# Weight loads of the last two chunks' second layer issued by SyncE instead of ScalarE

## The chip, the cores and the metric

The kernel runs on one core of a Trainium2 chip. The metric is the time of one execution on the device in microseconds. TensorE (PE) multiplies matrices; VectorE (DVE), ScalarE (ACT) and GpSimd (POOL) work element by element; ScalarE and SyncE (SP) also issue the transfers between the chip's main memory and its on-chip memory, each in its own order of instructions.

## The reference

The kernel computes a memory attention and, on its output, a token and channel mixer, all in 32-bit floating point. Cut to what matters:

```python
k_m = einsum("bhsm,bhsd->bhmd", softmax(phi, axis=2), k)      # likewise v_m from v
attn_out = softmax(q @ k_m.T / sqrt(64)) @ v_m                # 8 batches, 8 heads, 576 rows of 64
x = attn_out as (8, 576, 512)
h = relu(x.T @ w_tok1) @ w_tok2                               # over the 576 rows, 256 wide
u = x + h.T
out = u + relu(u @ w_ch1) @ w_ch2                             # over the 512 channels, 1536 wide
```

The change touches the last line, `relu(u @ w_ch1) @ w_ch2`, for the last two ninths of the rows.

## The kernel before

The 8 x 576 = 4608 rows are cut into nine chunks of 512, numbered 0 to 8. For each chunk the channel mixer has a first layer (512 channels to 1536 hidden values) and a second layer (back to 512). To keep 32-bit accuracy each operand is split into a high and a low part, and each product is three matmuls: high by high, high by low, low by high. The attention of later batches is computed between the channel mixer's matmuls of earlier chunks; nearly all of it is written out in the program's own order, so that every engine's instructions stand in the order in which the Python code emits them.

Chunks 0 to 2 are computed plainly. Chunks 3 to 6 take their first layer in quarters by a scheme with seven products instead of eight. The last two chunks, 7 and 8, are taken together, as a "double chunk", with both layers in that scheme. The seven products have the names "11", "21", "T2", "T1", "T3", "22", "T4", in this order.

The weights for these products are read from main memory, where an earlier part of the kernel has put them as sums of quarters. One transfer of 128 x 1024 values (512 KB), a "unit", holds the weights of two of the twelve hidden pieces of one product. The second layer of the double chunk takes 7 x 3 = 21 units, here numbered 0 to 20 (in the built program, unit_7313 is unit 0, unit_7689 is 18, unit_7711 is 19 and unit_7725 is 20). `load_unit(n)` makes a unit's tile and issues its load. The tile comes from a ring with the tag "c1", which units share with some of the hidden pieces: a load waits for the last reader of what its slot held.

The loop over `i` and `p` (L2267 to L2285) emits this second layer: for each product `name` and each hidden piece `p`,

- `double.piece` makes the split of a later hidden piece (`y` or `yT`), by a cast on ScalarE (L449, or a ReLU at L140) and a subtraction on VectorE (L450 or L143), and for T3 and T4 first a subtraction on VectorE (L439, L441);
- `load_unit(m0 + i * G + p // 2 + AHEAD)`, for every second `p`, issues the load of the unit three ahead;
- `double.second` emits the six matmuls (L456) of this piece into two of the four PSUM accumulators `e`;
- at `p == 1`, `gather` adds the accumulators that an earlier product has finished to the output tile on VectorE (L2260) and, where a half of a chunk's output is complete, stores it from SyncE (L219).

The calls of this loop load units 3 to 20. Units 0 to 2 are loaded from the first layer's loop (L2213). Product T4 comes after the loop (L2291 to L2302): it runs in three parts into the banks `end0` (512 rows of chunk 7), `end1` and `end2` (256 each), with units 18, 19 and 20 in each, and each part is added to the output (L2301) and stored (L2302).

The pieces of T4, the gathers of products T3 and T1 and the store of half of chunk 8 all come at the end of the loop. On VectorE the six T4 pieces stand ahead of these gathers, since `made` runs up to ten pieces ahead.

Of the kernel before, what the change touches and what calls it, by code (L numbers as in the profile page):

```python
# [28 lines left out]
def kernel(  # L29
# [25 lines left out]
    nc = tc.nc  # L55
# [10 lines left out]
    NF = 2 * w_ch2.shape[0]  # L66
# [9 lines left out]
    WIN, AHEAD = 3, 3  # L76
# [52 lines left out]
    def f32(t):  # L129
        return t.bitcast(F32)  # L130
# [435 lines left out]

    units = {}

    def load_unit(n):
        m = n - 2 * NF * (DOUBLE - WIN + 1)  # L570
        if m >= 7 * NF // 4:
            return
        p, j = n // 4 % (NF // 2), n % 4
        t = sb.tile([P, 1024], F32R, tag="c1", name=f"unit{n}", bufs=NF)
        if m >= 0:
            units[n] = t.rearrange("p (o x m) -> p o x m", o=2, x=2)
            nc.scalar.dma_start(out=f32(t), in_=Sums2.to[:, m // (NF // 4), m % (NF // 4)])
            return
        units[n] = t.rearrange("p (o x a n) -> p o x a n", o=2, x=2, a=2)
        m = 512 if j == 3 else 1024  # L580
        nc.scalar.dma_start(out=f32(t)[:, :m], in_=sums[p].to[:, j, :m])
# [1391 lines left out]
    while starts[-1][:2] != (B - 1, 1):  # L1973
        b, Q, m, r = starts[-1]
# [89 lines left out]
    for n in range(AHEAD):  # L2064
        at(2 * NF * WIN - 4 + n, load_unit, n, k=1)
# [50 lines left out]
    def quarters(c, p):  # L2116
# [22 lines left out]
        def product(ps, k, name, first):  # L2139
            if not k % 2:  # L2140
                load_unit(n + k // 2 + AHEAD)
            ch.product(ps, units[n + k // 2][:, k % 2], name, first, name in ("21", "22", "T4"))
# [59 lines left out]
    for p in range(NF // 2):  # L2202
        h, n = 2 * NF * DOUBLE + 4 * p, n0 + 4 * p
# [7 lines left out]
        def product(ps, k, name, first):  # L2211
            if not k % 2:
                load_unit(n + k // 2 + AHEAD)  # L2213
            double.product(ps, units[n + k // 2][:, k % 2], name, first, name in ("21", "22", "T4"))
# [34 lines left out]
    G = NF // 4  # L2249
# [4 lines left out]
    m0 = n0 + 2 * NF  # L2254
    after = []

    def gather(t, m, ps, store):
        for a in range(2):
            o = oc[t].o[:, 2 * m + a]
            nc.vector.tensor_tensor(out=o, in0=ps[a], in1=o, op=ALU.add)  # L2260
        if store:
            oc[t].store(channels=slice(2 * m, 2 * m + 2))
# [4 lines left out]
    for i, name in enumerate(double.order[:-1]):  # L2267
        y = name in ("21", "T1", "22")
        for p in range(NF // 2):
            k = i * (NF // 2) + p  # L2270
            while made[0] <= min(k + (6 if k < NF // 2 else 10), len(pieces) - 1):
                double.piece(*pieces[made[0]])
                made[0] += 1
            if not p % 2:
                load_unit(m0 + i * G + p // 2 + AHEAD)
            for a in range(2):
                double.second(
                    chain[y][a], a, name, p, units[m0 + i * G + p // 2][:, p % 2],
                    p == 0 and name in ("11", "21", "T1"), p == NF // 2 - 1,
                )  # L2280
            if p == 1:
                for x in after:
                    gather(*x)
                after.clear()
        after += [(t, m, chain[y], z) for t, m, z in ends[i]]  # L2285
# [100 lines left out]
```

## Time and profile before

| What | Value |
|---|---|
| median of 3 runs | 750.62 us (749.58 to 751.95) |
| profiled execution, whole | 751.26 us |
| its span in the profile | 749.5 us |
| ScalarE busy | 343.5 us (46%) |
| loads at L577 (second layer's units), issued by ScalarE | 21 of 512 KB |

The span is what the profile shows of the execution. Names such as `unit<-sums` are the program's tiles without their numbers: the target, an arrow, the source. `sums` is the store of weight sums in main memory, `u` the output tiles of chunks 7 and 8. PEld is TensorE's weight load, which runs beside the matmuls; ACTq and SPq are the instruction queues of ScalarE and SyncE, where transfers are issued. A row of the timeline gives start and duration in microseconds, then engine, line, operation, target and source, sizes, how many were merged into the row, and in brackets the idle time before it and what ended it. Merged rows overlap.

### The profile page before, as it was taken

To read this page: it belongs to the slowest core of one execution; us is meant where nothing else is said; L and a number is where in the kernel's file an instruction comes from. 1 tells how busy PE (TensorE), PEld (TensorE's weight loads), DVE (VectorE), ACT (ScalarE), POOL (GpSimd) and SP (SyncE) were. 2 spreads that over 40 slices of the span, in tenths; PEclk is the share of its full clock that TensorE was granted. 3 is DMA by queue.
4 is the path that set the end of the run, shared out by engine and by line. 5 is a ranking of instruction groups with operands and counts; after the bars stand their busy time and mean duration, and the time that the engine had idled before them with its cause. 6 is when DMAs were issued, how large, how long until landed. Compare 5 with 4: busy or idle time off the path is not lost.

```text
span 749.5 us, 12863 instructions
## 1 busy us (share of the span) xinstructions
PE 738.3 (99%) x4883; PEld 631.4 (84%) x4883; DVE 514.5 (69%) x920; ACT 343.5 (46%) x740; POOL 104.7 (14%) x90
## 2 busy tenths in 40 slices
PE   9999999999999999999999999999999999999997
PEld 8677788787878888898898889889898998888886
DVE  4989884787657768875577748675766555655874
ACT  5897554242314243545354536354444452444430
POOL 2134443012032021120010102010101000000000
PEclk9999999999999999999999999999999999999999
DMA  8945630584824554879596968878577555776654
GB/s 346 414 183 199 224 120 1 133 259 145 276 67 115 211 140 140 284 223 321 170 293 215 285 229 233 288 225 309 158 235 213 198 151 174 254 251 211 223 170 169
DMA packets 98462, 158.34 MB, mean 211 GB/s; under 512 B 42208, under 2 KB 65632, under 8 KB 94304
## 3 DMA queue, kind: packets, MB, share of 16 engines
q1 hardware_dynamic: 77808, 91.05, 36.8%
q10 hardware_dynamic: 20592, 66.46, 27.7%
q8 instruction: 39, 0.64, 0.3%
q14 instruction: 23, 0.19, 0.1%
HBM read 121.57 MB, written 35.91 MB: 210 GB/s over the span
## 4 chain that ended last, share of the span: by engine, by line
PE 57%; DVE 8%; DMA 5%; ACT 2%; SPq 1%; issue 1%; POOL 0%; ACTq 0%; DVEq 0%; POOLq 0%
PE acc L198 18%; PE qa L336 7%; PE qb L336 5%; PE u L937 5%; PE e L456 4%; PE da L401 4%; PE db L401 3%; PE cp L175 3%; PE Ap L897 2%; DMA rows<-S 1%; DMA raw<-rows 1%; PE sp L755 1%; PE sp L656 1%; PE end L456 1%; DMA sums<-c1h 1%; DMA sums<-sums 1%
## 5 line engine op out<-in xcount | busy, mean ns | idle before, releaser
L198 PE MATMUL acc<-qhh,c 128*128 128x512 f32 x256 | 99.8, 395 | 0.0
L198 PE MATMUL acc<-hh,c 128*128 128x512 f32 x288 | 96.5, 394 | 0.0
L336 PEld LDWEIGHTS qa<-xT,unit 128*128 128x128 f32 x432 | 60.7, 188 | 8.6 <-ACT whole L2134 2.9
L336 PEld LDWEIGHTS qb<-x,unit 128*128 128x128 f32 x432 | 60.9, 188 | 8.2 <-ACT whole L2134 2.2
L198 PEld LDWEIGHTS acc<-hh,c 128*128 128x128 f32 x288 | 54.1, 188 | 14.1 <-issue 2.7
L336 PE MATMUL qa<-xT,unit 128*128 128x256 f32 x432 | 63.5, 282 | 0.8 <-ACT whole L2134 0.7
L336 PE MATMUL qb<-x,unit 128*128 128x256 f32 x432 | 63.2, 282 | 0.9 <-ACT whole L2134 0.9
L2137 DVE TENSOR_TENSOR whole<-whole 128x256 f32<-128x256 f32 x48 | 26.1, 543 | 52.4 <-ACT whole L2134 52.1
L828 POOL TENSOR_TENSOR a<-aT,a 64x576 fp32r<-64x576 f32 x22 | 33.5, 1523 | 175.0 <-ACT a L827 152.3
L198 PE MATMUL acc<-hl,c 128*128 128x512 f32 x144 | 56.2, 390 | 0.0
L198 PEld LDWEIGHTS acc<-qhh,c 128*128 128x128 f32 x256 | 48.2, 188 | 9.2 <-issue 3.3
L198 PE MATMUL acc<-qal,c 128*128 128x512 f32 x192 | 54.7, 394 | 0.0
L2134 ACT COPY whole<-qa 128x256 f32<-128x256 f32 x72 | 26.9, 374 | 53.4 <-PE qa L336 44.9
L175 PE MATMUL cp<-uh,c1h 128*128 128x512 f32 x144 | 51.3, 397 | 0.0
L198 PE MATMUL acc<-qhl,c 128*128 128x512 f32 x128 | 50.8, 396 | 0.0
L175 PE MATMUL cp<-ul,c1h 128*128 128x512 f32 x144 | 50.3, 390 | 0.0
L175 PE MATMUL cp<-uh,c1l 128*128 128x512 f32 x144 | 50.2, 389 | 0.0
L143 DVE SCALAR_TENSOR_TENSOR hl<-cp,hh 128x512 fp32r<-128x512 f32 x36 | 24.7, 687 | 36.5 <-ACT hh L140 36.4
L198 PEld LDWEIGHTS acc<-qal,c 128*128 128x128 f32 x192 | 32.3, 189 | 3.0
L140 ACT ACTIVATE hh<-cp 128x512 fp32r<-128x512 f32 x36 | 21.5, 597 | 26.1 <-PE cp L175 26.0
L937 PE MATMUL u<-w2h,Rl 128*128 128x288 f32 x112 | 33.0, 295 | 0.3 <-DVE Rl L143 0.3
L2134 ACT COPY whole<-qb 128x256 f32<-128x256 f32 x48 | 17.8, 370 | 33.9 <-PE qb L336 33.7
(284 smaller groups left out, 1713.3 us busy)
## 6 DMA issues: line engine op xcount, KB each, us to landing
unit<-sums ACTq DMA_DIRECT2D x111, 512.0 KB, 4.2
kv<-in_kv_dram SPq DMA_DIRECT2D x12, 1280.0 KB, 8.0
rawc<-in_w_ch_dram SPq DMA_DIRECT2D x12, 1024.0 KB, 10.1
q<-in_q_dram SPq DMA_DIRECT2D x16, 576.0 KB, 7.3
unit<-sums ACTq DMA_DIRECT2D x30, 256.0 KB, 3.7
sums<-sums SPq DMA_DIRECT2D x12, 512.0 KB, 6.1
sums<-v SPq DMA_DIRECT2D x12, 512.0 KB, 5.5
phi<-in_phi_dram SPq DMA_DIRECT2D x16, 320.0 KB, 3.9
```

The lines of the kernel that those rows point to most:

```text
L140: nc.scalar.activation(out=h, in_=ps, func=AF.Relu)
L143: nc.vector.scalar_tensor_tensor(out=l, in0=ps, scalar=0.0, in1=f32(h), op0=ALU.max, op1=ALU.subtract)
L175: nc.tensor.matmul(ps, l[:, a, w], r[:, a], start=n == 0, stop=n == len(mm) - 1)
L198: nc.tensor.matmul(ps, l_[f // 2][:, f % 2, a * P : (a + 1) * P], r[:, w], start=f == start and x == 0, stop=f == end - 1 and x == 2,)
L336: nc.tensor.matmul(ps[:, :HW], l, r, start=first and n == 0, stop=n == len(mm) - 1, skip_group_check=not first,)
L401: nc.tensor.matmul(ps, l, r, start=first and n == 0, stop=n == len(mm) - 1, skip_group_check=not first,)
L456: nc.tensor.matmul(ps, weights[:, x, m], r[:, w], start=first and n == 0, stop=last and n == 2, skip_group_check=name in ("T2", "T3", "22"),)
L828: s.low_eng.tensor_tensor(out=l, in0=s.aT[own], in1=f32(h), op=ALU.subtract)
L897: nc.tensor.matmul(ps[:, :TT], a, w, start=x == 0, stop=x == len(mm) - 1)
L937: nc.tensor.matmul(ps[:, :HALF], a, r, start=x == 0, stop=x == len(mm) - 1)
L2134: nc.scalar.copy(out=to, in_=ps[:, :HW])
L2137: nc.vector.tensor_tensor(out=to, in0=x, in1=y, op=ALU.add)
```

## The change

`load_unit` gets a second argument, the engine that issues the load, with ScalarE as the default. The loop of the double chunk's second layer passes SyncE. All other calls keep ScalarE. The 18 loads of units 3 to 20 thus move from ScalarE's order into SyncE's.

```diff
-    def load_unit(n):
+    def load_unit(n, eng=nc.scalar):
         m = n - 2 * NF * (DOUBLE - WIN + 1)
...
         if m >= 0:
             units[n] = t.rearrange("p (o x m) -> p o x m", o=2, x=2)
-            nc.scalar.dma_start(out=f32(t), in_=Sums2.to[:, m // (NF // 4), m % (NF // 4)])
+            eng.dma_start(out=f32(t), in_=Sums2.to[:, m // (NF // 4), m % (NF // 4)])
             return
...
             if not p % 2:
-                load_unit(m0 + i * G + p // 2 + AHEAD)
+                load_unit(m0 + i * G + p // 2 + AHEAD, nc.sync)
```

SyncE's order at the end of the program; L577 are the moved loads, L219 the stores of the output, with u_6145 for chunk 7 and u_6179 for chunk 8:

```order
+L577 DMA unit_7647<-sums_101 128x1024
+L577 DMA unit_7668<-sums_101 128x1024
+L577 DMA unit_7689<-sums_101 128x1024
+L219 DMA out_dram<-u_6179 128x1024
+L577 DMA unit_7711<-sums_101 128x1024
+L577 DMA unit_7725<-sums_101 128x1024
+L219 DMA out_dram<-u_6179 128x1024
 L219 DMA out_dram<-u_6145 128x256
```

Units 19 and 20 stand between the two stores of chunk 8 (128x1024 each), which were neighbours before. Units 3 to 9 stand further up, ahead of the store of chunk 7's first half, and units 10 to 18 between that store and the first one shown.

ScalarE's order at the same place, with the casts of the T4 pieces (yT_7_7643, yT_7_7664, yT_7_7685) and the two last stores of chunk 7:

```order
 L449 CAST yT_7_7643<-r_7_6902 128x512
-L577 DMA unit_7647<-sums_101 128x1024
 L449 CAST yT_7_7643<-r_7_7006 128x512
 L449 CAST yT_7_7664<-r_7_7079 128x512
-L577 DMA unit_7668<-sums_101 128x1024
 L449 CAST yT_7_7664<-r_7_7155 128x512
 L449 CAST yT_7_7685<-r_7_7227 128x512
-L577 DMA unit_7689<-sums_101 128x1024
 L449 CAST yT_7_7685<-r_7_7294 128x512
-L577 DMA unit_7711<-sums_101 128x1024
-L577 DMA unit_7725<-sums_101 128x1024
 L219 DMA out_dram<-u_6145 128x512
```

Before, units 19 and 20 stood behind all six casts; now only the casts and the stores are left there. The order on TensorE, VectorE and GpSimd is the same in both programs; a few of the moved units and pieces take another slot of their ring.

## The prediction

> **What bounds the kernel now.** I read the page first, then TensorE's waits, then the chain of waits and the timeline of the last 30 us, since only the end of the program is touched.
>
> ```profile
> span 749.5 us, 12863 instructions
> PE 738.3 (99%) x4883; PEld 631.4 (84%) x4883; DVE 514.5 (69%) x920; ACT 343.5 (46%) x740; POOL 104.7 (14%) x90
> ```
>
> TensorE is busy for 738.3 of 749.5 us, so the change can gain only where TensorE stands still, and it loses as soon as TensorE has to stand still longer. In the touched stretch there is one such place in TensorE's waits:
>
> ```profile
> PE end L456 <- DMA unit<-sums: 1.3, 1, 1.3
> ```
>
> The chain of waits (start, duration, what) has the same place on the path that sets the end:
>
> ```profile
> 733.69 5.00 DMA unit<-sums
> 738.68 0.14 issue
> 738.82 7.33 PE end L456 x48
> 746.14 0.02 issue
> 746.17 0.42 DVE u L2301
> ```
>
> A weight unit is issued at 733.69 and has landed at 738.68; 0.14 us later TensorE begins its last 48 matmuls, and everything up to the end of the span hangs on them. Which unit it is follows from TensorE's order: stage "T4" reads units 18, 19, 20, and the first six of its 54 matmuls need unit 18 alone. So 48 are left when it waits for unit 19. Before this, nothing is missing (columns: window, its length, busy PE, PEld, DVE, ACT, POOL, granted clock, DMA share, GB/s):
>
> ```profile
> 727.80:736.00 8.20, 8.20 (x38) 6.79 (x37) 5.60 (x9) 2.36 (x4) 0.00 (x0) 1.00 0.56 149
> 736.00:738.80 2.80, 1.48 (x7) 0.92 (x6) 2.56 (x5) 0.00 (x0) 0.00 (x0) 1.00 0.97 383
> ```
>
> TensorE is full up to 737.48 (736.00 + 1.48) and then waits 1.34 us. That is all that a better delivery of these units could bring.
>
> **What leaves ScalarE costs it nothing and gains nothing.** Eighteen issues go. Here are the last ones beside the casts of the six T4 pieces (the bracket is the idle time and what ended it):
>
> ```profile
> 723.70 0.62 ACT L449 CAST yT<-r 128x512 fp32r<-128x512 f32 x1 [2.64 <-DVE r L441]
> 723.70 0.33 ACTq L577 DMA_DIRECT2D unit<-sums  x1
> 725.68 0.63 ACT L449 CAST yT<-r 128x512 fp32r<-128x512 f32 x1 [1.36 <-DVE r L441]
> 727.67 0.62 ACT L449 CAST yT<-r 128x512 fp32r<-128x512 f32 x1 [1.36 <-DVE r L441]
> ...
> 731.70 0.33 ACTq L577 DMA_DIRECT2D unit<-sums  x1
> 733.62 0.62 ACT L449 CAST yT<-r 128x512 fp32r<-128x512 f32 x1 [1.36 <-DVE r L441]
> 733.69 0.81 ACTq L577 DMA_DIRECT2D unit<-sums  x2
> ```
>
> An issue takes 0.33 us, but it runs beside the cast: the casts follow each other at 1.98 us with an issue between them (723.70 to 725.68) and at 1.99 without (725.68 to 727.67). What each cast waits for is VectorE. So the 18 x 0.33 = 5.9 us leave an engine that was waiting anyway. I cost them at 0.
>
> **Units 3 to 18 on SyncE.** In the new order SyncE has nothing else to wait for ahead of units 3 to 9, and one store ahead of units 10 to 18:
>
> ```profile
> 704.24 40.55 SPq L219 DMA_DIRECT2D out_dram<-u  x4
> 704.95 0.33 ACTq L577 DMA_DIRECT2D unit<-sums  x1
> ```
>
> ```profile
> 686.96:695.12 8.16, 8.16 (x37) 6.76 (x37) 6.26 (x11) 6.00 (x11) 0.00 (x0) 1.00 0.67 194
> 719.60:727.80 8.20, 8.20 (x37) 6.77 (x37) 6.23 (x10) 2.54 (x5) 0.00 (x0) 1.00 0.53 166
> ```
>
> That store (of chunk 7, channels 0 and 1) goes out at 704.24, and unit 10 was issued on ScalarE at 704.95, so the store holds nothing back. Units 3 to 9 wait for the same matmuls as on ScalarE, their slots' readers, and go no later. A stage of three units takes 8.16 us of TensorE from 686.96 on, so unit m is first read at 686.96 + 2.72 m: unit 10 at 714.2. A unit can be loaded once its slot has been read by the last reader: unit 18 has the slot of the first T3 piece, which TensorE reads in the first sixth of stage T3, up to 719.6 + 1.4 = 721.0. ScalarE issued unit 18 only at 731.7, behind the casts. It now lands some 10 us earlier, but TensorE did not wait for it. Cost and gain 0. The cover is 3 us or more for each unit even at the longest landing seen (6.5 us, below): 704.6 + 6.5 = 711.1 against 714.2.
>
> **Units 19 and 20 on SyncE: the term that counts.** In SyncE's new order a store of chunk 8 (channels 0 and 1) stands between unit 18 and unit 19. It waits for four additions on VectorE (L2260), which stand behind the T4 pieces:
>
> ```profile
> 734.28 0.69 DVE L450 TENSOR_TENSOR yT<-r,yT 128x512 fp32r<-128x512 f32 x1 [0.69 <-ACT yT L449]
> 734.89 3.67 DVE L2260 TENSOR_TENSOR u<-e,u 128x512 f32<-128x512 f32 x6
> 737.39 1.53 SPq L219 DMA_DIRECT2D out_dram<-u  x2
> 737.39 0.35 SPq L219 DMA_DIRECT2D out_dram<-u  x1
> ```
>
> Six additions take 3.67 us, the fourth ends at 734.89 + 4 x 0.61 = 737.33, and the store is issued at 737.39. Nothing in the change moves these additions: the chain of six pieces ahead of them begins with work released by TensorE, which is full. So in the new kernel unit 19 is issued at 737.39 + 0.35 + the gap between two issues (0.81 for two on ScalarE, so some 0.08) = **737.8 instead of 733.69**, and unit 20 at 738.25 instead of 734.1. The slot of unit 19, that of the second T3 piece, is free from about 719.6 + 2 x 1.4 = 722.4; it is the store in front that holds the unit. Queued behind the waiting store are units 19 and 20 and the next store; TensorE waits for the units, nobody for that store.
>
> Then the landing. The new kernel has unit 19 as the second of two 512 KB transfers issued back to back on one queue. Two pairs of that kind are there (the answer for line 577 in windows around each pair; first the issues, then the times to landing, minimum, median, maximum):
>
> ```profile
> L577 ACTq DMA_DIRECT2D unit<-sums x2: 327/386/444, 683.1 to 683.5; - x2
> DMA to landing us min/median/max: 3.6/4.1/4.5
> ```
>
> ```profile
> L577 ACTq DMA_DIRECT2D unit<-sums x2: 326/386/445, 733.7 to 734.1; - x2
> DMA to landing us min/median/max: 5.0/5.4/5.8
> ```
>
> ```profile
> L577 ACTq DMA_DIRECT2D unit<-sums x21: 326/326/445, 679.0 to 734.1; - x21
> DMA to landing us min/median/max: 3.4/3.8/6.5
> ```
>
> The second of a pair took 4.5 and 5.8 us; all 21 such loads lie between 3.4 and 6.5. The later pair came 2 us after unit 18, and stores joined it at 737.39; at 737.8 no load is under way, so I stay near the quiet pair and take 4.8. No row shows a load right behind a store, hence the full bounds. Unit 19 lands at 737.8 + 4.8 = 742.6, TensorE restarts 0.14 later at 742.74 instead of 738.82: **+3.9 us**. With 3.4 it is +2.5, with 6.5 +5.6. Unit 20 adds nothing of weight: in the quiet pair the second lands 0.4 + 4.5 - 3.6 = 1.3 us after the first, and the six matmuls on unit 19 take about as long (1.48 us of busy time for the first six in the window above).
>
> By the Trainium skill ("DMA: Bandwidth & Descriptors", section "Issuing engines are not separate DMA queues"), the queues of different engines run on the same 16 DMA engines, and another issuing engine saves only issue time; by that the sum would be 0. The trace agrees that issue time is all that ScalarE gives up (0.33 us each), but the rule does not speak of what stands ahead in the issuer's own order.
>
> **Sum.** 0 + 0 + 3.9: the span goes from 749.5 to 753.4, and the profiled execution, 751.26 with what lies around its span, to 755.2. The three runs have a median of 750.62, so I forecast 754.5.
>
> **Rivals.**
> *A colder TensorE.* The pause grows from 1.34 to 742.74 - 737.48 = 5.3 us, longer than any in the trace after the start. At the start, after idling, the same 128x128 matmul was slower for a while (the start on the timeline, then line 1278 in two windows, then the whole core in two windows):
>
> ```profile
> 1.57 5.62 PE L1278 MATMUL pp<-ident 128*128 128x128 f32 x30 [1.57 <-POOL mask L105]
> ```
>
> ```profile
> L1278 PE MATMUL pp<-ident x6: 421/421/421, 4.3 to 5.4; 128*128 128x128 f32 x6
> L1278 PE MATMUL pp<-ident x7: 275/275/275, 6.2 to 6.9; 128*128 128x128 f32 x7
> ```
>
> ```profile
> 3.00:6.00 3.00, 3.00 (x17) 3.00 (x16) 1.96 (x4) 1.61 (x3) 0.00 (x0) 1.00 0.93 353
> 6.00:9.00 3.00, 3.00 (x29) 3.00 (x28) 0.32 (x2) 0.95 (x4) 0.00 (x0) 1.00 0.93 319
> ```
>
> From 1.57 (the first matmul) to about 5.4 it ran 17 matmuls in 3 us, later 29, though the granted clock reads 1.00 in both. If the pause brings that back, 3.8 us at 17/29 of the pace lose 3.8 x 12/29 = 1.6 us: +5.5, or 756.1. For it: 5.3 us is as long as that spell. Against it: after 1.34 us nothing of the kind is seen, and no longer pause is there to judge by.
> The Trainium skill ("TensorE: Matmul & The Clock Gate", section "HAM oscillation — how this bites in real kernels") says that an idle gap of more than about 3.4 us puts TensorE back to half its clock; whether a free-running window falls whole into the gap is left to chance. The slow start agrees with it; no pause in this trace tests it.
>
> *No change.* If SyncE handed unit 19 on without being held by the store, it would go as its slot allows and land well before 737.48 or about where it does now: 749.3 to 750.6. Against it stands a row of SyncE's waits (us in total, times, the longest):
>
> ```profile
> SPq L219 <- DVE u L2260: 34.8, 3, 17.8
> ```
>
> Before one of these stores SyncE stood for 17.8 us and issued nothing.
>
> *The other side, faster.* Without the issues in its order, ScalarE might run the six T4 casts sooner, so that VectorE's four additions end earlier. Break-even needs unit 19 landed at 738.68, so issued at 733.9 and the fourth addition ended at 733.4, 3.9 us earlier than now; from there on it gains, to at most 1.34 us (749.3). The pitch of 1.98 us is 0.69 + 0.63 + 0.69 less the overlap, with or without an issue, so the six pieces hold no 3.9 us to give.
>
> **How the numbers follow.** Forecast as summed 0.53, the colder TensorE 0.33, no change 0.09, faster 0.05. The forecast's own range is +2.5 to +5.6, so 753.1 to 756.2; the colder case adds 1.6 to it and reaches up to 757.8. I leave out its last 0.6 us, and go 0.5 below the lower end for the scatter of the runs: 752.6 to 757.2 leaves out no change, faster and a thin top, together under 0.2. About 0.3% (2.3 us) is what a measurement of this kernel can tell from no change, so the borders are 748.4 and 752.9. Slower: 0.53 + 0.33, less 0.02 for a fast landing, gives 0.84. Faster: even the whole 1.34 us stays inside the border, so of the 0.05 only 0.02 is left for it. Within: the rest, 0.14.
>
> **What would show it.** In the profile of the changed kernel, unit 19's issue on SyncE should directly follow the store at about 737.4, and TensorE's wait "end <- DMA unit" should be 4 to 7 us instead of 1.3. ScalarE's casts at L449 should keep their pitch of 1.98 us. The 48 matmuls should take 7.33 us; 8.5 or more would be the colder TensorE. The prediction is wrong if unit 19 is issued before 736, if its landing is outside 3.4 to 6.5 us, or if TensorE shows a new wait ahead of T4.

## The result and the profile after

| | kernel before | kernel after |
|---|---|---|
| median | 751.99 us (749.58 to 753.85, 6 runs) | 759.64 us (758.05 to 761.3, 6 runs) |
| profiled execution, whole | 751.26 us | 758.05 us |
| its span | 749.5 us | 756.3 us |
| mean granted clock of TensorE | 1.000 | 0.995 |

The change makes the kernel slower: ratio 1.010, 95% interval 1.0081 to 1.0118, that is 6 to 9 us. In three of the experiments below (e1, e6 and e7) one execution each took far longer than the rest (4141, 903 and 812 us); the ratios leave these out. The forecast was 754.5 us in a range that ended at 757.2. The span grows by 6.8 us, and the profile shows all of it at one place. First the page of the kernel after: the span, TensorE's busy time and the granted clock in 40 slices, and under it the clock row of the kernel before:

```profile
span 756.3 us, 12877 instructions
PE 741.1 (98%) x4883; PEld 634.4 (84%) x4883; DVE 513.9 (68%) x920; ACT 342.3 (45%) x740; POOL 103.9 (14%) x90
...
PEclk9999999999999999999999999999999999999997
```

```profile
PEclk9999999999999999999999999999999999999999
```

The busy time of TensorE is 2.8 us longer for the same 4883 matmuls, and the clock digit of the last slice is 7 where it was 9 before. The rest is waiting. The chain of waits of the kernel after, from VectorE's fourth addition on (start, duration, what):

```profile
736.51 0.69 DVE u L2260
737.20 0.02 issue
737.22 0.34 SPq L219
737.55 0.05 issue
737.60 0.03 SPq L577
737.63 0.03 issue
737.66 5.50 DMA unit<-sums
743.16 0.14 issue
743.29 9.65 PE end L456 x48
```

This is the predicted sequence, step by step: the addition ends, SyncE issues the store of chunk 8, then unit 19 at 737.66, and only when that has landed does TensorE go on. Before, unit 19 was issued at 733.69 and TensorE went on at 738.82: 4.47 us lost. And the last 48 matmuls take 9.65 us instead of 7.33: 2.3 us more. The sum, 6.8, is the whole growth of the span. The windows of the kernel after around the pause say why the matmuls are slower (window, length, busy PE, PEld, DVE, ACT, POOL, granted clock, DMA share, GB/s):

```profile
741.00:741.50 0.50, 0.00 (x0) 0.00 (x0) 0.00 (x0) 0.00 (x0) 0.00 (x0) 1.00 1.03 328
741.50:742.00 0.50, 0.00 (x0) 0.00 (x0) 0.00 (x0) 0.00 (x0) 0.00 (x0) 0.53 1.25 238
...
748.00:748.20 0.20, 0.20 (x2) 0.10 (x2) 0.00 (x0) 0.00 (x0) 0.00 (x0) 0.50 0.00 0
748.20:748.40 0.20, 0.20 (x2) 0.20 (x1) 0.00 (x0) 0.00 (x0) 0.00 (x0) 0.62 0.00 0
748.40:748.60 0.20, 0.20 (x3) 0.16 (x3) 0.00 (x0) 0.00 (x0) 0.00 (x0) 1.00 0.00 0
```

In the middle of the pause, at about 741.5, the granted clock falls from 1.00 to 0.50, and it comes back at about 748.3. So the first 5.0 us behind the pause (743.29 to 748.3) run at half the clock. (It falls once more at 755.2, behind the last matmul, where it costs nothing.) The mean clock was 0.995 or 0.996 in all six runs of the kernel after, so this was no accident of the profiled one.

### The profile page after: what moved, and what is told of

Read it like the earlier page. It is cut to its first block, busy times and chain, and to the rows that moved or that the text cites. A ratio compares the mean times of both kernels' runs of the same rounds, so it can differ in the third digit from the quotient of the medians.

```text
span 756.3 us, 12877 instructions
## 1 busy us (share of the span) xinstructions
PE 741.1 (98%) x4883; PEld 634.4 (84%) x4883; DVE 513.9 (68%) x920; ACT 342.3 (45%) x740; POOL 103.9 (14%) x90
## 4 chain that ended last, share of the span: by engine, by line
PE 57%; DVE 8%; DMA 5%; ACT 3%; SPq 1%; issue 1%; POOL 0%; ACTq 0%; DVEq 0%; POOLq 0%
PE acc L198 18%; PE qa L336 7%; PE u L937 5%; PE qb L336 5%; PE e L456 4%; PE da L401 4%; PE db L401 3%; PE cp L175 3%; PE Ap L897 2%; PE end L456 1%; DMA raw<-rows 1%; DMA rows<-S 1%; PE sp L755 1%; PE sp L656 1%; DVE whole L2137 1%
## 5 line engine op out<-in xcount | busy, mean ns | idle before, releaser
L937 PE MATMUL u<-w2h,Rh 128*128 128x288 f32 x112 | 33.1, 295 | 0.0
```

The source lines that it names most:

```text
L937: nc.tensor.matmul(ps[:, :HALF], a, r, start=x == 0, stop=x == len(mm) - 1)
```

## The experiments

The theory: SyncE's order, in which units 19 and 20 stand behind a store that waits for VectorE, makes the pause; and the pause halves the clock. The rivals: it is SyncE's queue, or the move of all 18 loads, that costs the time; and the lower clock has another cause than the pause.

The start of T4 differs by up to 5 us between profiles, though TensorE's order is the same up to there (735.1 to 740.3 us), so the table below gives the **tail**, from the first matmul of T4 to the end of the span, beside the ratio of times to the kernel before. The tail is 749.5 - 735.96 = 13.5 us in the kernel before and 756.3 - 735.82 = 20.5 in the kernel after.

| kernel | ratio of times, 95% interval | pause before unit 19 (e5: 20) | last matmuls | tail |
|---|---|---|---|---|
| before | | 1.3 us | 48 in 7.3 us | 13.5 us |
| after | 1.010 (1.0081 to 1.0118) | 5.95 | 9.6 | 20.5 |
| e1, e1b: 19, 20 back on ScalarE | 0.998 (0.9964 to 1.0000) | none | | 12.1 |
| e2: only 19, 20 moved | 1.010 (1.0068 to 1.0138) | 5.9 | 9.3 | 20.1 |
| e3, e3b: the store on ScalarE | 0.9993 (0.9973 to 1.0013), 0.9988 (0.9964 to 1.0012) | none | | 12.0, 12.1 |
| e4: pause filled | 1.009 (1.0062 to 1.0114) | 1.05 | 7.3 | 18.2 |
| e5: only 20 behind the store | 1.006 (1.0036 to 1.0087) | 3.9 | 42 in 8.3 | 19.0 |
| e6: a small store ahead | 1.006 (1.0032 to 1.0088) | 4.3 | 9.5 | 18.5 |
| e7: all on ScalarE, store too | 1.010 (1.0067 to 1.0127) | 6.05 | 9.3 | 20.2 |
| e8: pause half filled | one run | 2.98 | 8.9 | 19.7 |

### Which loads cost the time: e1, e1b and e2

```diff
-                load_unit(m0 + i * G + p // 2 + AHEAD, nc.sync)
+                load_unit(m0 + i * G + p // 2 + AHEAD, nc.sync if i * G + p // 2 + AHEAD < 19 else nc.scalar)
```

> Units 3 to 18 on SyncE, units 19 and 20 back on ScalarE. Theory (the store ahead of units 19 and 20 in SyncE's order makes the pause, and the pause lowers TensorE's clock): unit 19 is issued near 733.6 as before, TensorE waits 1.3 us (1 to 2), the 48 last matmuls take 7.3 us, the time is that of the kernel before within 1 us. Rival (it is the move of loads to SyncE as such: its queue delivers more slowly, or the other slots hurt): most of the 7 us stays, 5 us or more above the kernel before.

> The kernel of e1 once more, for a profile of an undisturbed execution. Theory: from the first matmul of T4 to the end of the span 13.5 us as in the kernel before, unit 19 issued behind the last cast as before, a pause of 1 to 2 us, granted clock 1.0. Rival (the move of units 3 to 18 costs something): a new wait of TensorE ahead of T4, or a longer tail.

e2 has the two engines exchanged (`nc.scalar if ... < 19 else nc.sync`).

> Units 3 to 18 on ScalarE as before, only units 19 and 20 on SyncE. Theory: the whole loss, 6.5 to 8 us above the kernel before, with unit 19 issued at 737.7, a pause of about 6 us and 9.6 us for the 48 matmuls. Rival (the move of all loads): 2 us or less, a ninth of the loads being moved.

With units 19 and 20 back on ScalarE the loss is gone; with these two alone on SyncE it is whole. The sixteen other loads cost nothing. e2's waits of TensorE and the end of its chain repeat those of the kernel after:

```profile
PE end L456 <- DMA unit<-sums: 5.9, 1, 5.9
...
742.12 5.45 DMA unit<-sums
747.71 9.36 PE end L456 x48
```

One thing in e1b was not expected by anyone: TensorE does not wait at all. Its timeline, and the answer for line 577 in the window of unit 19's issue:

```profile
734.40 0.81 ACTq L577 DMA_DIRECT2D unit<-sums  x2
736.68 8.79 PE L456 MATMUL end<-yT,unit 128*128 128x512 f32 x54
```

```profile
L577 ACTq DMA_DIRECT2D unit<-sums x1: 326/326/326, 734.4 to 734.4; - x1
DMA to landing us min/median/max: 3.7/3.7/3.7
```

The 54 matmuls of T4 run as one piece. Unit 19 is still issued behind the last cast, but lands in 3.7 us instead of 5.0. Unit 18, which ScalarE had issued 2 us earlier in the kernel before, has here long landed (SyncE issued it as soon as its slot was free), so unit 19 does not have it ahead. e5 below shows the same from the other side: there unit 18 goes out 2.0 us ahead of unit 19, but unit 20 not right behind it; unit 19 lands in 3.8 us, and TensorE stands still for less than 0.2 us. So by these two profiles the old pause of 1.3 us was the price of three loads close together.

### The store or the queue: e3, e3b and e7

e3 and e3b keep all 18 loads on SyncE and let ScalarE issue the two stores of chunk 8. e7 does the same to the stores in the kernel before, where all loads are on ScalarE: none of these loads and neither of these two stores is on SyncE then, but the order "store, unit 19, unit 20" is the one of the change.

```diff
-            oc[t].store(channels=slice(2 * m, 2 * m + 2))
+            oc[t].store(channels=slice(2 * m, 2 * m + 2), eng=(nc.sync, nc.scalar)[t])
```

> All 18 units on SyncE as in the change, but the two stores of chunk 8 are issued by ScalarE. Theory: unit 19 is issued when its slot is free, about 722.4, TensorE does not wait for it at all; span about 748.2, 1.3 us below the kernel before, 8 us below the change. Rival (SyncE's queue delivers more slowly): the wait stays at several us and the time near that of the change.

> The kernel of e3 once more, against the kernel before, since its first interval (0.9973 to 1.0013) holds both no change and the expected gain. Theory: 1.3 us of pause are gone, ratio 0.9982, tail from the first matmul of T4 to the end of the span 12.0 us against 13.5. Rival (the gain is given back elsewhere): ratio 1.000 or more with a new wait ahead of T4.

> No load moved: all 21 units on ScalarE as before, but the two stores of chunk 8 are issued by ScalarE too, the first ahead of units 19 and 20. Theory (it is the order behind a waiting store, whatever the engine): the loss of the change again, unit 19 issued near 737.7, a pause near 6 us, the clock at 0.5 behind it, 6.5 to 8 us above the kernel before. Rival (SyncE's queue is the cause): the time of the kernel before.

e7 is as slow as the change without a single load on SyncE, with the same pause (its waits, its timeline, and the landing of units 19 and 20):

```profile
PE end L456 <- DMA unit<-sums: 6.1, 1, 6.1
```

```profile
736.53 0.38 ACTq L219 DMA_DIRECT2D out_dram<-u  x1
737.02 1.19 ACTq L577 DMA_DIRECT2D unit<-sums  x2
738.31 14.48 ACTq L219 DMA_DIRECT2D out_dram<-u  x3
742.69 9.26 PE L456 MATMUL end<-yT,unit 128*128 128x512 f32 x48 [6.05 <-DMA unit<-sums]
```

```profile
L577 ACTq DMA_DIRECT2D unit<-sums x2: 367/574/782, 737.0 to 737.4; - x2
DMA to landing us min/median/max: 5.5/6.0/6.4
```

And e3, with every load on SyncE and the store out of the way, has no pause (its timeline):

```profile
720.33 3.52 SPq L577 DMA_DIRECT2D unit<-sums  x4
736.46 8.55 PE L456 MATMUL end<-yT,unit 128*128 128x512 f32 x54
```

The last four loads are issued between 720.3 and 723.8, long before they are read, and T4 runs through. The last two, issued 0.3 us apart, take 6.1 and 6.9 us to land, so e3 alone does not clear SyncE's queue of being slow; it only takes the wait away. But behind the store unit 19 takes the same 5.5 us to land from ScalarE's queue (e7) as from SyncE's (kernel after). So what counts here is not which engine's queue it is, but what stands ahead in it. Of the expected gain of 1.3 us the tail shows 1.4 to 1.5 (12.0 and 12.1 against 13.5). In the times it is not proven: both intervals hold no change as well as a gain of 0.2%. e3 and e1 are the versions that no other one beats; "as fast as the kernel before, perhaps 1 us faster" is what the runs allow to say.

### The clock: e4, e5 and e8

e4 puts 22 matmuls into the pause; their result is never read. e8 puts 13 there.

```diff
             if x == 0 and p == 1:
+                idle = pch.tile([P, CW], F32, tag="ch", name="idle", bufs=2)
+                for n in range(22):
+                    nc.tensor.matmul(
+                        idle, units[m0 + 6 * G][:, 0, 0, :P], double.y["T4", 0][0],
+                        start=n == 0, stop=n == 21,
+                    )
                 for z in after:
```

> The change with 22 more matmuls (of unit 18, into a bank that nobody reads) between the six matmuls on unit 18 and those on unit 19, 5.0 us of work at full clock that ends before unit 19 lands. Theory (the lower clock comes from the pause): unit 19 lands at about 743.2 as in the change, but the 48 matmuls behind it take 7.3 us instead of 9.6 at a granted clock of 1.0; time 2.3 us below the change, 4.5 to 5.5 above the kernel before. Rival (the lower clock belongs to the late end of the program or to the transfers beside it, not to the pause): 9.6 us and the time of the change. Were the 22 matmuls in the way, TensorE would show no idle time before unit 19.

> Only unit 20 on SyncE, behind the store of chunk 8; unit 19 stays on ScalarE. A test of how long a pause must be. Order alone: unit 19 lands a little later than 738.7 at most, unit 20 is issued at 737.7 and lands 4.5 to 5.5 us later; TensorE works 1.4 us on unit 19 and pauses up to about 742.5 to 743.2, a second pause of some 3 us after the first of 1.3. If the clock goes down for any pause of more than about 3 us, the matmuls behind it run at 0.5 and the tail from the first matmul of T4 is 13.5 + 2.8 + 2.3 = 18.6 us; if it needs one pause of 3.4 us or more without a matmul, the clock stays at 1.0 and the tail is about 16.3 us.

> As e4, with 13 instead of 22 more matmuls (2.95 us of work), so that the pause before unit 19 is about 3.0 us: between the 1.05 and 1.3 us that left the clock alone and the 3.9 us that did not. In the four profiles where it fell, it fell 2.2 to 4.2 us after the last matmul. If a fall needs a whole window of 3.4 us without a matmul, the clock stays at 1.0 and the 48 matmuls take 7.33 us; if it goes by a mean over a window, it may fall already, and they take 9 us or more.

The timeline of e4, and the last 6 us of its matmuls as a window:

```profile
738.87 5.15 PE L2300 MATMUL idle<-yT,unit 128*128 128x512 f32 x22
...
745.07 7.33 PE L456 MATMUL end<-yT,unit 128*128 128x512 f32 x48 [1.05 <-DMA unit<-sums]
```

```profile
746.40:752.40 6.00, 6.00 (x44) 5.48 (x42) 1.12 (x2) 0.00 (x0) 0.00 (x0) 1.00 0.24 85
```

Unit 19 comes as late as in the change (5.59 us from issue to landing), but the clock stays at 1.00 and the 48 matmuls take 7.33 us. The tail is 2.3 us shorter than that of the change, as expected. The time did not follow as closely: 1.0088 is 6.6 us, where 4.5 to 5.5 were expected, but its interval begins at 4.7. In all eight executions of e4 the mean clock is 0.998 or more, in all six of the kernel after 0.995 or 0.996. The lower clock belongs to the pause.

e5 (its edit is that of e2 with `== 20` in place of `< 19`, the engines in e1's order) leaves unit 19 on ScalarE and has its pause before unit 20, 3.9 us long. The clock fell: the tail is 19.0 us, near the 18.6 expected for that case. Its waits, and windows in and behind the pause:

```profile
PE end L456 <- DMA unit<-sums: 3.9, 1, 3.9
...
743.10:744.80 1.70, 0.00 (x0) 0.00 (x1) 0.00 (x0) 0.00 (x0) 0.00 (x0) 0.52 0.99 405
744.80:750.00 5.20, 5.17 (x18) 4.62 (x19) 0.69 (x1) 0.00 (x0) 0.00 (x0) 0.50 0.20 74
```

This holds for the profiled execution. In e5's ten executions the mean clock lies between 0.945 and 0.999: two have 0.999, while half the clock for 3.4 us, the shortest spell seen here, would take 0.002 off the mean. So the clock did not go down like this in every one of them; how long the pause was in those two is not recorded.

e8, a single execution, goes below the 3.4 us that I had named as a bound, with a pause of 2.98 us, and the clock fell as well. Its timeline, and windows behind the pause:

```profile
747.68 8.88 PE L456 MATMUL end<-yT,unit 128*128 128x512 f32 x48 [2.98 <-DMA unit<-sums]
```

```profile
747.70:748.40 0.70, 0.70 (x3) 0.62 (x4) 0.00 (x0) 0.00 (x0) 0.00 (x0) 1.00 1.03 421
748.50:751.80 3.30, 3.30 (x9) 2.57 (x8) 0.00 (x0) 0.00 (x0) 0.00 (x0) 0.50 0.26 104
751.90:756.00 4.10, 4.10 (x35) 4.06 (x34) 1.12 (x2) 0.00 (x0) 0.00 (x0) 1.00 0.23 83
```

Here TensorE was already at work again, at full clock, for 0.7 us before the clock fell. So a whole window of 3.4 us without a matmul is not needed. The trace of e2 has a still shorter case, far from the end of the program and from the weight units of T4: at 465.07 TensorE restarts after 2.30 us of waiting for ScalarE (its wait, two times and 3.3 us in all, the longest 2.3), and from 465.4 to 468.8 the clock is at 0.50:

```profile
PE Ap L897 <- ACT nat L136: 3.3, 2, 2.3
...
465.40:468.70 3.30, 3.12 (x15) 2.90 (x14) 3.24 (x8) 1.33 (x4) 0.42 (x1) 0.50 0.94 373
```

In the profiles pauses of up to 1.93 us (e8, at 589.2) left the clock alone, and all from 2.30 us on lowered it. No run was made to find the bound between them.

### The landing: e6

```diff
-        if store:
+        if store and t and m:
+            oc[t].store(w=slice(0, 128), channels=slice(2, 3))
+        elif store:
             oc[t].store(channels=slice(2 * m, 2 * m + 2))
...
             if x == 0 and p == 1:
+                oc[1].store(w=slice(128, CW), channels=slice(2, 3))
+                oc[1].store(channels=slice(3, 4))
```

> The change, with the store ahead of units 19 and 20 cut down to its first 128 of 1024 columns (64 KB); the rest of it is stored after unit 20. The wait in SyncE's order is the same, the data ahead is an eighth. Theory A (the landing of 5.5 us holds the transfer of the 512 KB store ahead): unit 19 issued at 737.7, landing 4.2 to 4.6 us, pause about 5 us. Theory B (5.5 us is what a pair of loads takes at this place anyway, as 5.0 did before): landing 5.0 to 5.5, pause near 6 us. In both the time stays 5 us or more above the kernel before, since the wait for the additions stays.

The small store waits for one addition fewer, so it and unit 19 were issued earlier: unit 19 1.24 us after the start of T4 instead of 1.84. The landing is in the answer for line 577 of e6, beside that of the kernel after (both for units 19 and 20 together):

```profile
L577 SPq DMA_DIRECT2D unit<-sums x2: 372/397/422, 736.5 to 737.0; - x2
DMA to landing us min/median/max: 4.4/5.0/5.6
```

```profile
L577 SPq DMA_DIRECT2D unit<-sums x2: 372/574/777, 737.7 to 738.1; - x2
DMA to landing us min/median/max: 5.5/5.9/6.3
```

Unit 19 lands in 4.4 us with 64 KB ahead and in 5.5 with 512 KB: the 448 KB that are gone from ahead of it are worth 1.1 us, as theory A had it. The pause is 4.3 instead of 5.95 us; 1.1 of the difference come from the landing and 0.6 from the earlier issue, which neither theory had. The clock falls all the same. The time is 4.5 us above the kernel before, a little under the 5 us or more that both theories expected.

## Why the prediction was wrong

- **What bounds the end, and the sign: right.** The pause before unit 19 on the path that sets the end, and the path behind it, are there unchanged, only later.
- **Nothing gained or lost on ScalarE: right.** The casts keep their pitch: 723.55, 725.53 and 727.51 in the kernel after.
- **Units 3 to 18 at 0: right for the change, not as a statement on the loads.** e1b shows that taking unit 18 out of the way is worth the whole old pause of 1.3 us. In the change nothing of this is left, since units 19 and 20 go later for another reason. "TensorE did not wait for it" was true of unit 18, but unit 19 did.
- **Unit 19 issued at 737.8: right** (737.66), and e2, e3 and e7 show that the store ahead is the cause. The prediction called it the store of channels 0 and 1 of chunk 8; it is that of channels 2 and 3, which are added first, and it is the fourth addition that it waits for, as said.
- **The landing: mis-sized.** The step "I stay near the quiet pair and take 4.8" should have gone to the upper of its two pairs: 5.5 us were measured, and TensorE restarted 4.47 us later instead of 3.9. The quiet pair was wrong in kind: the transfer ahead of unit 19 was a store, and by e6 seven eighths of its data cost 1.1 us.
- **The clock: the step that failed.** The prediction had the mechanism as the rival "a colder TensorE" and gave it 0.33, with "after 1.34 us nothing of the kind is seen, and no longer pause is there to judge by". In every profile here with a pause of 2.30 us or more the clock fell. The prediction's own sign for this rival, 8.5 us or more for the 48 matmuls, came out at 9.65. The forecast left the cost out of its sum, and the range stopped at 757.2, short even of the rival's own upper end of 757.8. The rival's price, 1.6 us, was too low as well: 2.3 measured. It was taken from the slow start of the kernel, 3.8 us at 17/29 of the pace; the spell here had 5.0 us left at half the clock.
- By sizes: 3.9 forecast; 0.6 more from unit 19 (0.7 from its landing, less 0.14 since it was issued a little earlier than forecast) and 2.3 from the clock make 6.8, the growth of the span. The six runs of the kernel before have a median 1.4 us above the three that the forecast started from, which puts the measured median still further up.
- **The rivals "no change" and "faster" fell**: the store held the loads, and the fourth addition ended at 737.20 against 737.33.

## What to carry to other kernels

A transfer that is issued early only needs a free slot, but its engine issues in order: before moving a load to another engine, look for the one instruction ahead of it there that waits longest, and move that instead. In the profiles of this kernel a pause of TensorE of 2.3 us or more cost more than its length, since part of the work behind it ran at half the clock; a forecast that lengthens a pause to that size should carry this in the sum, not among the rivals. And how long a load takes to land depends on what goes out close to it (unit 19 took 3.7 us in e1b, 5.0 before and 5.5 after), so issuing its neighbours at another time can be worth more than issuing it sooner.

## What the hardware showed

The granted clock changes on a grid. By windows of 0.1 us, it fell at 741.5, 745.3, 743.2, 739.1 and 740.1 us (the kernel after, e2, e5, e6, e7) and came back 6.83 us later each time. Where TensorE was already at work when it fell, it came back after half of that, 3.41 us: 748.5 to 751.9 in e8 and 465.4 to 468.8 in e2. All changes within one trace lie a whole number of 3.41 us apart, also a last fall behind the last matmul (755.2 in the kernel after, 758.9 in e2); from 465.38 to 745.28 in e2 there are 82 such steps. The fall came 2.2 to 4.2 us after the pause began, so it does not follow a fixed delay. In the 3.41 us just ahead of each fall that follows a pause, TensorE had stood still for 2.25 us or more (2.25 in e5 and e6, 2.30 in e2 at 465, 2.63 in e8); behind e2's last matmul 1.89 us were enough. The pause of 1.93 us in e8 that left the clock alone lies on both sides of a grid point (47 steps ahead of 748.46), 0.8 us before it and 1.1 us behind. So what seems to count is how long TensorE stands still within one step of the grid, not the whole pause; no run was made to test this. The Trainium skill ("TensorE: Matmul & The Clock Gate", section "HAM oscillation — how this bites in real kernels") has the fall for idle gaps of more than about 3.4 us. The half clock agrees with these runs, the bound does not: 2.98 us was enough in e8 and 2.30 us in e2. The loss comes to nearly half of what is left of the spell when TensorE restarts: 5.0 / 2 = 2.5 us against 2.3 measured in the kernel after, 4.7 / 2 = 2.35 against 2.2 in e6.
